# Two token tiles of the second batch turned on TensorE, and two GpSimd products moved ahead of five loads

## The chip, the cores and the metric

The kernel runs on one core of a Trainium2 chip. The metric is the device time of one execution in microseconds (us); lower is better. The core's engines are TensorE (PE in the profile; PEld is its weight loads), VectorE (DVE), ScalarE (ACT), GpSimd (POOL) and SyncE (SP, which only issues DMAs here). Each engine runs its own list of instructions in order and waits on semaphores for the others.

## The reference

Sliding-window attention with sink tokens, followed by a gated block over the whole sequence. There are 4 batches, 8 heads, 768 tokens, 64 values a head; each query sees the 127 keys before it, itself, and the first 4 keys.

```python
# attention, per batch and head
scores = (q @ k.T) / sqrt(64)
keep = (pos_k < 4) | ((pos_q - pos_k >= 0) & (pos_q - pos_k < 128))
a = softmax(where(keep, scores, -1e9))
x = a @ v                                  # heads side by side: (4, 768, 512)
# gated block
h = gelu_tanh(x @ w_in)                    # (4, 768, 1024)
u, v = h[..., :512], h[..., 512:]
v_n = (v - mean(v)) / sqrt(var(v) + 1e-6) * g_ln
v_s = einsum('ts,bsd->btd', w_sg, v_n) + b_sg[None, :, None]
out = x + (u * v_s) @ w_out
```

## The kernel before

All work is cut into small steps, each a Python function with a short name, and one string, `STEPS`, writes out by hand the order in which the steps are recorded. Each step puts its instructions at the end of its engine's list, so the string fixes the order on each engine and, between engines, what can overlap. A step reads `NAME.batch.index...`; a last letter A, D or P chooses ACT, DVE or POOL. The four batches are interleaved: while the gated block of one batch runs, the attention of the next runs beside it, and the loads of the one after that arrive.

A batch has 6 tiles of 128 tokens. The steps around the change are these (lines are those of the profile):

- `LQ`, `LK` (line 223) and `LVH` (line 272): loads of q, k and v, issued by GpSimd, converting to bf16. `LK.3.0` is the first token tile of k of batch 3; `LVH.2.0` is half of the heads of v of batch 2.
- `TK`, `EK` (lines 379, 197): k turned on TensorE, and copied from PSUM. `DQ`, `DK` (line 437): q and k turned by a transposing DMA that SP issues, two token tiles each.
- `QK.b.p.g` (line 480): scores of head pair p and token tiles 2g and 2g+1, into one of two score buffers (`sc`) in PSUM. `EX` (line 485): the exponential on ACT. `MK` (lines 492, 495, 498): the window mask, on DVE or, as two selects, on POOL.
- `AV.b.p.k` (lines 521, 525, 528): the value product of head pair p for half k of the tokens (three tiles), into one of four `mm` buffers in PSUM. `NR` (lines 537, 538): the division by the row sum, which writes `x_sb` in bf16.
- `XT`, `XE` (lines 547, 197): two token tiles of x turned on TensorE, eight 128x128 transposes into an `mm` buffer, then copied to `xT`. Batch 0 uses these throughout. `XD` (line 554): half of x, three token tiles, turned by a transposing DMA that SP issues. Batches 1 to 3 use it.
- `MV.b.g` (line 563): the product with the v half of `w_in` for token tiles 2g and 2g+1, into a score buffer; `GV` (line 567) its GELU. `MU`, `GU` (lines 607, 612): the same for the u half. `TL` (line 570): a tiny ACT instruction that has the GELU's table loaded.
- `BN`, `RS`, `NM`, `Z` (lines 579 to 583, 588, 591, 597, 600): mean and variance, the inverse root (on POOL), the offset, and the normalised tile.
- `SP.b.h.c` (line 627): the product over tokens with `w_sg`; `GT` (line 632) scale and bias on DVE; `GM` (line 637) the gate product u * v_s, on DVE or POOL.
- `OU` (line 644): the product with `w_out`; `RA` (line 648) the residual sum; `ST` (line 667) the store.

Buffers turn in rings: a step that takes a buffer waits until the last reader of its use before is done. Four `mm` buffers serve `AV`, `XT`, `TK`, `SP`, `SK` and `OU` in the order of recording; two `sc` buffers serve `QK`, `MV` and `MU`.

For batch 1, `XD.1.0` turns tiles 0 to 2 once `NR.1.0.0` to `NR.1.3.0` have written them, and `XD.1.1` turns tiles 3 to 5 once `NR.1.0.1` to `NR.1.3.1` have. `MV.1.0` and `MU.1.0` need tiles 0 and 1, `MV.1.1` tiles 2 and 3. In the order around the change, PE runs the value products `AV.1.0.1` to `AV.1.3.1`, the scores `QK.2.2.0` and `QK.2.3.0`, the output products `OU.0.1` and `OU.0.2`, then `MV.1.0`. SP issues `XD.1.0`, `XD.1.1`, then `DQ.2.1`, `DQ.2.2`, `DK.2.2`, `DK.3.0`, `DQ.3.0`.

Of the kernel before, what the change touches and what calls it, by code (L numbers as in the profile page):

```python
# [43 lines left out]
NM.1.1 Z.1.0.A LK.3.3 RS.1.2 OU.0.3 GU.1.2 NM.1.2 Z.1.1.D Z.1.2.D Z.1.4.D Z.1.3.A Z.1.5.D OU.0.4 QK.2.0.1 QK.2.1.1
RA.0.3 DK.3.0 SP.1.0.0 RA.0.4 EX.2.0.1 SP.1.0.1 SK.2.0 GT.1.0.0 DQ.3.0 EX.2.1.1 SX.2.0 GM.1.0.0.D SP.1.1.0 MK.2.0.1.P
GT.1.0.1 QK.2.2.1 ST.0.3 GT.1.1.0 QK.2.3.1 GM.1.0.1.P EX.2.2.1 AV.2.0.0 SP.1.1.1 MK.2.1.1.D EX.2.3.1 MK.2.2.1.P
NR.2.0.0 AV.2.1.0 QK.2.0.2 QK.2.1.2 EX.2.0.2 MK.2.3.1.P NR.2.1.0 SP.1.1.2 GT.1.1.1 EX.2.1.2 OU.0.5 MK.2.0.2.P GT.1.1.2
ST.0.0 ST.0.4 QK.2.2.2 RA.0.5 QK.2.3.2 MK.2.1.2.P EX.2.2.2 AV.2.2.0 AV.2.3.0 NR.2.2.0 SP.1.1.3 EX.2.3.2 NR.2.3.0
QK.3.0.0 MK.2.3.2.P QK.3.1.0 GT.1.1.3 XD.2.0 EX.3.0.0 AV.2.0.1 MK.2.2.2.D AV.2.1.1 EX.3.1.0 NR.2.0.1 AV.2.2.1
GM.1.1.3.P ST.0.1 NR.2.1.1 AV.2.3.1 ST.0.2 ST.0.5 GM.1.1.0.P NR.2.2.1 QK.3.2.0 QK.3.3.0 NR.2.3.1 EX.3.2.0 GM.1.1.2.P  # L50
SP.1.0.2 EX.3.3.0 XD.2.1 DQ.3.1 DK.3.1 SP.1.0.3 GT.1.0.2 MK.3.3.0.D MV.2.0 GM.1.0.2.P GM.1.1.1.D LK.3.4 LK.3.5 LQ.3.4
LQ.3.5 MK.3.0.0.D OU.1.3 LVH.3.0 GV.2.0 OU.1.4 RA.1.3 LVH.3.1 DK.3.2 DQ.3.2 OU.1.5 ST.1.3 RA.1.4 GT.1.0.3 MV.2.1 ST.1.4
MK.3.1.0.D KS.3 BN.2.0 GM.1.0.3.P MV.2.2 GV.2.1 BN.2.1 MU.2.1 GV.2.2 BN.2.2 RS.2.1 MU.2.0 GU.2.1 NM.2.1 RA.1.5 RS.2.2
MU.2.2 GU.2.0 NM.2.2 Z.2.4.D Z.2.5.D Z.2.0.A Z.2.1.D OU.1.0 GU.2.2 Z.2.2.D MK.3.2.0.D OU.1.1 RA.1.0 Z.2.3.D QK.3.0.1
QK.3.1.1 RA.1.1 SP.2.0.0 EX.3.0.1 EX.3.1.1 OU.1.2 MK.3.0.1.P GT.2.0.0 ST.1.5 VSM.3 ST.1.0 QK.3.2.1 ST.1.1 QK.3.3.1
EX.3.2.1 SP.2.1.0 GM.2.0.0.D MK.3.1.1.P RA.1.2 EX.3.3.1 SP.2.0.1 ST.1.2 MK.3.3.1.P QK.3.0.2 GT.2.0.1 QK.3.1.2 SK.3.0
EX.3.0.2 SX.3.0 SP.2.1.1 GT.2.1.0 MK.3.2.1.P EX.3.1.2 GM.2.1.0.D SP.2.1.2 GT.2.1.1 GM.2.0.1.D AV.3.0.0 MK.3.1.2.P
GT.2.1.2 AV.3.1.0 NR.3.0.0 AV.3.2.0 AV.3.3.0 MK.3.0.2.P NR.3.1.0 QK.3.2.2 QK.3.3.2 EX.3.2.2 SP.2.0.2 NR.3.2.0 NR.3.3.0
EX.3.3.2 SP.2.0.3 MK.3.2.2.P GT.2.0.2 XD.3.0 AV.3.0.1 GT.2.0.3 MK.3.3.2.P AV.3.1.1 NR.3.0.1 AV.3.2.1 GM.2.0.3.P
NR.3.1.1 AV.3.3.1 SP.2.1.3 GM.2.0.2.D GM.2.1.1.P NR.3.2.1 OU.2.0 NR.3.3.1 GT.2.1.3 XD.3.1 OU.2.1 RA.2.0 GM.2.1.3.P  # L60
OU.2.2 GM.2.1.2.D ST.2.0 RA.2.1 MV.3.0 RA.2.2 ST.2.1 OU.2.3 GV.3.0 OU.2.4 BN.3.0 MV.3.1 RA.2.3 RA.2.4 MV.3.2 ST.2.3
GV.3.1 ST.2.2 ST.2.4 BN.3.1 OU.2.5 GV.3.2 MU.3.2 BN.3.2 RS.3.1 MU.3.1 GU.3.2 NM.3.1 RS.3.2 NM.3.2 Z.3.0.D Z.3.1.A
MU.3.0 Z.3.2.D Z.3.3.A Z.3.4.A Z.3.5.D RA.2.5 ST.2.5 SP.3.1.0 GU.3.0 SP.3.1.1 GU.3.1 GT.3.1.0 SP.3.1.2 GM.3.1.0.D
# [11 lines left out]
def kernel(  # L75
# [474 lines left out]
        copy(e, xT.get(b)[:, 2 * g:2 * g + 2].rearrange("p t c i -> p (t c) i"), ps16(("x", b, g), 8))  # L550

    def XD(b, half):
        ts = slice(3 * half, 3 * half + 3)
        return nc.sync.dma_start_transpose(out=xT.get(b)[:, ts, :, :].rearrange("p t c i -> p (t c) i"),
                                           in_=x_sb[b][:, ts, :].rearrange("p t d -> p (t d)"))

# [159 lines left out]
```

## Time and profile before

| | |
|---|---|
| median of 3 runs | 156.38 us (155.83 to 157.84) |
| the profiled execution's own time | 156.0 us |
| its span in the profile | 154.3 us |
| TensorE clock granted | 1.00 |
| busy: PE, DVE, ACT, POOL | 93%, 79%, 64%, 64% |
| DMA traffic | 25.44 MB, mean 165 GB/s |

The span is what the profile covers, from the first to the last instruction; the execution's own time has a little more around it. Busy shares are means over the whole span. In a timeline row the first number is the start in us from the span's start, the second the length in us, then engine, line and operation, output and inputs; a bracket at the end tells how long the engine stood idle before it and who ended that. Matmul records overlap, since matmuls are pipelined. Rows of SPq and of GpSimd's DMA instructions show the issue of a DMA, not the moving of its data; "DMA to landing" is counted from the start of the issue.

### The profile page before, as it was taken

What the parts mean: (1) busy time and instruction counts of PE and PEld (TensorE: products, weight loads), DVE (VectorE), ACT (ScalarE), POOL (GpSimd) and SP (SyncE); (2) the same over time, 40 slices, a digit from 0 to 9 for tenths busy, and PEclk for the clock granted to TensorE, in tenths of its full rate; (3) what the DMA queues carried; (4) which work ended last, traced back from release to release, by engine and by line L of the source; (5) the groups of instructions that cost most, each with busy time, mean ns of one, the idle gap of its engine ahead of it and who ended that gap; (6) DMA issues with size and microseconds to landing.
All of it is one profiled execution on the core that took longest, in us unless ns stands there. A gap on an engine that the chain in (4) does not pass through costs nothing.

```text
span 154.3 us, 3696 instructions
## 1 busy us (share of the span) xinstructions
PE 143.3 (93%) x1460; PEld 92.1 (60%) x1471; DVE 122.2 (79%) x292; ACT 99.4 (64%) x111; POOL 98.7 (64%) x127
## 2 busy tenths in 40 slices
...
GB/s 162 280 357 150 150 193 207 170 189 213 142 139 141 191 157 130 208 154 145 127 155 219 181 283 174 157 156 157 307 168 19 87 238 0 207 66 7 0 224 184
DMA packets 89337, 25.44 MB, mean 165 GB/s; under 512 B 81828, under 2 KB 86184, under 8 KB 89320
## 3 DMA queue, kind: packets, MB, share of 16 engines
...
q8 instruction: 11, 0.18, 0.5%
q14 instruction: 6, 0.05, 0.1%
...
## 4 chain that ended last, share of the span: by engine, by line
PE 72%; DMA 16%; DVE 4%; SPq 3%; POOL 2%; issue 1%; DVEq 0%
PE mm L627 17%; PE sc L607 14%; PE sc L563 13%; PE mm L644 12%; DMA k<-in_k_dram 6%; DMA z<-in_q_dram 5%; PE sc L480 4%; DMA xT<-x_sb 4%; PE mm L521 3%; SPq L243 3%; PE mm L525 2%; PE mm L379 2%; PE mm L528 1%; PE mm L619 1%; DVE x_sb L538 1%
## 5 line engine op out<-in xcount | busy, mean ns | idle before, releaser
L485 ACT ACTIVATE P<-sc 128x1024 bf16<-128x1024 f32 (+1 forms) x48 | 43.6, 956 | 9.3 <-PE sc L480 9.1
L627 PE MATMUL mm<-wsgT,z 128*128 128x384 bf16 x192 | 34.3, 327 | 0.0
L627 PEld LDWEIGHTS <-z 128*128 128x128 bf16 x192 | 17.5, 98 | 12.0 <-issue 1.2
L563 PE MATMUL sc<-w_in_sb,xT 128*128 128x512 bf16 x93 | 21.9, 379 | 1.5 <-DMA xT<-x_sb 1.3
L632 DVE SCALAR_TENSOR_TENSOR gtmp<-mm,g_sb,b_bc 128x384 bf16<-128x384 f32 x32 | 19.2, 611 | 4.5 <-PE mm L627 4.2
L644 PE MATMUL mm<-w_out_sb,wsg_gated 128*128 128x512 bf16 x89 | 22.0, 379 | 0.4
L607 PE MATMUL sc<-xT,w_in_sb 128*128 128x256 bf16 x192 | 22.1, 273 | 0.0
L495 POOL TENSOR_SCALAR_AFFINE_SELECT P<-P 128x512 bf16<-128x512 bf16 x21 | 13.7, 651 | 13.0 <-ACT P L485 12.3
L637 POOL TENSOR_TENSOR wsg_gated<-gtmp,uT 128x384 bf16<-128x384 bf16 x15 | 14.5, 986 | 10.5 <-DVE gtmp L632 10.5
L579 DVE BATCH_NORM_STATS2 st<-vt 128x6 f32<-128x512 f32 x24 | 15.4, 682 | 7.2 <-ACT vt L567 7.1
L607 PEld LDWEIGHTS <-w_in_sb 128*128 128x128 bf16 x192 | 18.7, 98 | 3.0
L567 ACT ACTIVATE vt<-sc 128x1024 f32<-128x1024 f32 x12 | 12.3, 1024 | 11.3 <-PE sc L563 11.3
L538 DVE TENSOR_TENSOR x_sb<-mm,rcp 128x384 bf16<-128x384 f32 (+1 forms) x36 | 18.5, 513 | 1.2
L648 DVE TENSOR_TENSOR ot<-mm,x_sb 128x512 f32<-128x512 f32 x24 | 16.1, 683 | 2.4 <-PE mm L644 2.4
L223 POOL DMA_DIRECT2D k<-in_k_dram x18 | 16.4, 921 | 1.1 <-DMA v_sb<-in_v_dram 1.1
L588 POOL TENSOR_TENSOR rs<-rs,neg_half 128x4 f32<-128x4 f32 (+1 forms) x8 | 6.9, 867 | 15.3 <-DVE rs L583 14.1
L521 PE MATMUL mm<-v_sb,P 128*128 128x65 bf16 x192 | 16.2, 194 | 0.4 <-DVE x_sb L538 0.3
L223 POOL DMA_DIRECT2D q<-in_q_dram x18 | 16.4, 928 | 0.0
L563 PEld LDWEIGHTS <-xT 128*128 128x128 bf16 x96 | 9.2, 98 | 11.9 <-DMA xT<-x_sb 1.8
L521 PEld LDWEIGHTS <-P 128*128 128x128 bf16 x192 | 14.6, 97 | 2.4 <-DMA v_sb<-in_v_dram 0.5
L525 PE MATMUL mm<-v_sb,P 128*128 128x65 bf16 x160 | 15.5, 193 | 0.4 <-POOL P L498 0.4
L480 PE MATMUL sc<-qT,kT 64*128 64x128 bf16 (+1 forms) x256 | 14.6, 238 | 1.0 <-DVE qT L198 0.6
...
## 6 DMA issues: line engine op xcount, KB each, us to landing
...
```

The source lines that it names most:

```text
L223: return nc.gpsimd.dma_start(out=dst.rearrange("p (h d) -> p h d", h=H), in_=heads(src, b, i))
L480: nc.tensor.matmul(sc[:, hl, c:c + 128 * ni], at(kT, b)[rows, j, p, :], at(qT, b)[rows, i:i + ni, p, :], start=not biased, stop=(not biase ...
L485: nc.scalar.activation(out=P.new((b, p, g))[:, :, 0:w], in_=sc_ring[b, p, g][:, :, 0:w], func=AF.Exp, scale=scale)
L521: nc.tensor.matmul(av[:, il, hl, :], pt[:, hl, c:c + 128], vb[:, h, i, :], start=first, stop=False)
L525: nc.tensor.matmul(av[:, il, hl, :], pt[:, hl, c:c + 128], vb[:, h, i - 1, :], start=False, stop=(i < 2 and il == n - 1 and hl == 1))
L538: nc.vector.tensor_mul(x_sb.get(b)[:, i0:i0 + n, 128 * p:128 * (p + 1)].rearrange("p t (h d) -> p t h d", h=2), av[:, :, :, 0:Dh], rcp[:, ...
L563: nc.tensor.matmul(hp[:, jl, :], xT[b][:, 2 * g + jl, c, :], w_in_sb[:, c, d_half:2 * d_half], start=(c == 0), stop=(c == KD - 1))
L607: nc.tensor.matmul(hp[:, dc // 2, 256 * (dc % 2):256 * (dc % 2 + 1)], w_in_sb[:, c, 128 * dc:128 * (dc + 1)], xT[b][:, 2 * g:2 * g + 2, c, :],
L627: nc.tensor.matmul(ps[:, 0:NH], z[b][:, si, 128 * dc:128 * (dc + 1)], wsgT[:, si, NH * hf:NH * (hf + 1)], start=(si == 0), stop=(si == NT ...
L632: nc.vector.scalar_tensor_tensor(out=gtmp.new((b, hf, dc)), in0=mm_ring["g", b, hf, dc][:, 0:NH], scalar=g_sb[:, dc:dc + 1], in1=b_bc[:, N ...
L644: nc.tensor.matmul(ps, gated(b, hf)[:, dc, 128 * tl:128 * (tl + 1)], w_out_sb[:, dc, :], start=(dc == 0), stop=(dc == KU - 1))
L648: nc.vector.tensor_add(ot.new((b, t)), mm_ring["o", b, t], x_sb[b][:, t, :])
```

## The change

In batch 1, token tiles 0 and 1 of x are turned by `XT.1.0` on TensorE and copied by `XE.1.0` on ACT, and `XD.1.0` turns tile 2 alone. `XD.1.1` still turns tiles 3 to 5. `XT.1.0` stands behind `QK.2.3.0`. Both score steps `QK.2.2.0` and `QK.2.3.0`, which stood behind `AV.1.3.1`, now stand ahead of it, as does `XT.1.0`. On ACT, `XE.1.0` stands between `EX.2.2.0` and `EX.2.3.0`. On GpSimd, the gate products `GM.0.1.3` and `GM.0.1.1` stand directly behind `GM.0.1.2` and ahead of `LK.3.0`, `LK.3.1`, `LQ.3.0`, `LQ.3.1` and `LVH.2.0`; before, they stood behind those and `LVH.2.1`. The orders of DVE and of SP's issues stay as they were.

```diff
 ...
-RA.0.0 AV.1.0.1 XD.1.0 EK.2.1.A MK.1.3.2.P AV.1.1.1 NR.1.0.1 AV.1.2.1 EX.2.1.0 GM.0.1.2.P NR.1.1.1 AV.1.3.1 NR.1.2.1
-QK.2.2.0 LK.3.0 LK.3.1 LQ.3.0 LQ.3.1 LVH.2.0 QK.2.3.0 EX.2.2.0 OU.0.1 NR.1.3.1 EX.2.3.0 TL OU.0.2 XD.1.1 DQ.2.1 DQ.2.2
-DK.2.2 RA.0.1 MK.2.3.0.D MV.1.0 VSM.2 MU.1.0 GV.1.0 MK.2.1.0.D LVH.2.1 GM.0.1.3.P GM.0.1.1.P BN.1.0 MV.1.1 GU.1.0
+RA.0.0 AV.1.0.1 XD.1.0 EK.2.1.A MK.1.3.2.P AV.1.1.1 NR.1.0.1 AV.1.2.1 EX.2.1.0 QK.2.2.0 QK.2.3.0 XT.1.0 EX.2.2.0
+GM.0.1.2.P NR.1.1.1 AV.1.3.1 NR.1.2.1 GM.0.1.3.P GM.0.1.1.P LK.3.0 LK.3.1 LQ.3.0 LQ.3.1 LVH.2.0 OU.0.1 NR.1.3.1
+XE.1.0.A EX.2.3.0 TL OU.0.2 XD.1.1 DQ.2.1 DQ.2.2 DK.2.2 RA.0.1 MK.2.3.0.D MV.1.0 VSM.2 MU.1.0 GV.1.0 MK.2.1.0.D LVH.2.1
+BN.1.0 MV.1.1 GU.1.0
 ...
     def XD(b, half):
-        ts = slice(3 * half, 3 * half + 3)
+        ts = slice(2 if b == 1 and half == 0 else 3 * half, 3 * half + 3)
         return nc.sync.dma_start_transpose(out=xT.get(b)[:, ts, :, :].rearrange("p t c i -> p (t c) i"),
                                            in_=x_sb[b][:, ts, :].rearrange("p t d -> p (t d)"))
```

From `BN.1.0` on, the written order is the same in both.

More of the change, by code (lines that the diff above doesn't have):

```diff
@@ L39 @@
 NR.1.1.0 AV.1.2.0 AV.1.3.0 MK.1.0.2.P GT.0.1.3 QK.2.0.0 QK.2.1.0 NR.1.2.0 EX.2.0.0 OU.0.0 MK.1.2.2.P NR.1.3.0 TK.2.1
-RA.0.0 AV.1.0.1 XD.1.0 EK.2.1.A MK.1.3.2.P AV.1.1.1 NR.1.0.1 AV.1.2.1 EX.2.1.0 GM.0.1.2.P NR.1.1.1 AV.1.3.1 NR.1.2.1
-QK.2.2.0 LK.3.0 LK.3.1 LQ.3.0 LQ.3.1 LVH.2.0 QK.2.3.0 EX.2.2.0 OU.0.1 NR.1.3.1 EX.2.3.0 TL OU.0.2 XD.1.1 DQ.2.1 DQ.2.2
-DK.2.2 RA.0.1 MK.2.3.0.D MV.1.0 VSM.2 MU.1.0 GV.1.0 MK.2.1.0.D LVH.2.1 GM.0.1.3.P GM.0.1.1.P BN.1.0 MV.1.1 GU.1.0
-LQ.3.2 RA.0.2 LQ.3.3 MK.2.0.0.D MV.1.2 GV.1.1 MK.2.2.0.D KS.2 BN.1.1 MU.1.1 GV.1.2 BN.1.2 LK.3.2 RS.1.1 MU.1.2 GU.1.1
@@ L44 @@
[L44 to L63, printed above, removed]
@@ L64 @@
-GT.3.1.1 SP.3.1.3 GM.3.1.1.D GT.3.1.2 SP.3.0.0 GM.3.1.2.D SP.3.0.1 GT.3.0.0 GT.3.1.3 SP.3.0.2 GT.3.0.1 GM.3.1.3.P
-SP.3.0.3 GM.3.0.0.D GM.3.0.1.P GT.3.0.2 OU.3.3 GM.3.0.2.D GT.3.0.3 OU.3.4 GM.3.0.3.D RA.3.3 OU.3.0 RA.3.4 ST.3.3 OU.3.1
-RA.3.0 ST.3.4 OU.3.2 ST.3.0 RA.3.1 OU.3.5 ST.3.1 RA.3.2 ST.3.2 RA.3.5 ST.3.5
+RA.0.0 AV.1.0.1 XD.1.0 EK.2.1.A MK.1.3.2.P AV.1.1.1 NR.1.0.1 AV.1.2.1 EX.2.1.0 QK.2.2.0 QK.2.3.0 XT.1.0 EX.2.2.0
+GM.0.1.2.P NR.1.1.1 AV.1.3.1 NR.1.2.1 GM.0.1.3.P GM.0.1.1.P LK.3.0 LK.3.1 LQ.3.0 LQ.3.1 LVH.2.0 OU.0.1 NR.1.3.1
@@ new lines @@
+XE.1.0.A EX.2.3.0 TL OU.0.2 XD.1.1 DQ.2.1 DQ.2.2 DK.2.2 RA.0.1 MK.2.3.0.D MV.1.0 VSM.2 MU.1.0 GV.1.0 MK.2.1.0.D LVH.2.1
+BN.1.0 MV.1.1 GU.1.0 LQ.3.2 RA.0.2 LQ.3.3 MK.2.0.0.D MV.1.2 GV.1.1 MK.2.2.0.D KS.2 BN.1.1 MU.1.1 GV.1.2 BN.1.2 LK.3.2
+RS.1.1 MU.1.2 GU.1.1 NM.1.1 Z.1.0.A LK.3.3 RS.1.2 OU.0.3 GU.1.2 NM.1.2 Z.1.1.D Z.1.2.D Z.1.4.D Z.1.3.A Z.1.5.D OU.0.4
+QK.2.0.1 QK.2.1.1 RA.0.3 DK.3.0 SP.1.0.0 RA.0.4 EX.2.0.1 SP.1.0.1 SK.2.0 GT.1.0.0 DQ.3.0 EX.2.1.1 SX.2.0 GM.1.0.0.D
+SP.1.1.0 MK.2.0.1.P GT.1.0.1 QK.2.2.1 ST.0.3 GT.1.1.0 QK.2.3.1 GM.1.0.1.P EX.2.2.1 AV.2.0.0 SP.1.1.1 MK.2.1.1.D
@@ new lines @@
+EX.2.3.1 MK.2.2.1.P NR.2.0.0 AV.2.1.0 QK.2.0.2 QK.2.1.2 EX.2.0.2 MK.2.3.1.P NR.2.1.0 SP.1.1.2 GT.1.1.1 EX.2.1.2 OU.0.5
+MK.2.0.2.P GT.1.1.2 ST.0.0 ST.0.4 QK.2.2.2 RA.0.5 QK.2.3.2 MK.2.1.2.P EX.2.2.2 AV.2.2.0 AV.2.3.0 NR.2.2.0 SP.1.1.3
+EX.2.3.2 NR.2.3.0 QK.3.0.0 MK.2.3.2.P QK.3.1.0 GT.1.1.3 XD.2.0 EX.3.0.0 AV.2.0.1 MK.2.2.2.D AV.2.1.1 EX.3.1.0 NR.2.0.1
+AV.2.2.1 GM.1.1.3.P ST.0.1 NR.2.1.1 AV.2.3.1 ST.0.2 ST.0.5 GM.1.1.0.P NR.2.2.1 QK.3.2.0 QK.3.3.0 NR.2.3.1 EX.3.2.0
+GM.1.1.2.P SP.1.0.2 EX.3.3.0 XD.2.1 DQ.3.1 DK.3.1 SP.1.0.3 GT.1.0.2 MK.3.3.0.D MV.2.0 GM.1.0.2.P GM.1.1.1.D LK.3.4
@@ new lines @@
+LK.3.5 LQ.3.4 LQ.3.5 MK.3.0.0.D OU.1.3 LVH.3.0 GV.2.0 OU.1.4 RA.1.3 LVH.3.1 DK.3.2 DQ.3.2 OU.1.5 ST.1.3 RA.1.4 GT.1.0.3
+MV.2.1 ST.1.4 MK.3.1.0.D KS.3 BN.2.0 GM.1.0.3.P MV.2.2 GV.2.1 BN.2.1 MU.2.1 GV.2.2 BN.2.2 RS.2.1 MU.2.0 GU.2.1 NM.2.1
+RA.1.5 RS.2.2 MU.2.2 GU.2.0 NM.2.2 Z.2.4.D Z.2.5.D Z.2.0.A Z.2.1.D OU.1.0 GU.2.2 Z.2.2.D MK.3.2.0.D OU.1.1 RA.1.0
+Z.2.3.D QK.3.0.1 QK.3.1.1 RA.1.1 SP.2.0.0 EX.3.0.1 EX.3.1.1 OU.1.2 MK.3.0.1.P GT.2.0.0 ST.1.5 VSM.3 ST.1.0 QK.3.2.1
+ST.1.1 QK.3.3.1 EX.3.2.1 SP.2.1.0 GM.2.0.0.D MK.3.1.1.P RA.1.2 EX.3.3.1 SP.2.0.1 ST.1.2 MK.3.3.1.P QK.3.0.2 GT.2.0.1
@@ new lines @@
+QK.3.1.2 SK.3.0 EX.3.0.2 SX.3.0 SP.2.1.1 GT.2.1.0 MK.3.2.1.P EX.3.1.2 GM.2.1.0.D SP.2.1.2 GT.2.1.1 GM.2.0.1.D AV.3.0.0
+MK.3.1.2.P GT.2.1.2 AV.3.1.0 NR.3.0.0 AV.3.2.0 AV.3.3.0 MK.3.0.2.P NR.3.1.0 QK.3.2.2 QK.3.3.2 EX.3.2.2 SP.2.0.2
+NR.3.2.0 NR.3.3.0 EX.3.3.2 SP.2.0.3 MK.3.2.2.P GT.2.0.2 XD.3.0 AV.3.0.1 GT.2.0.3 MK.3.3.2.P AV.3.1.1 NR.3.0.1 AV.3.2.1
+GM.2.0.3.P NR.3.1.1 AV.3.3.1 SP.2.1.3 GM.2.0.2.D GM.2.1.1.P NR.3.2.1 OU.2.0 NR.3.3.1 GT.2.1.3 XD.3.1 OU.2.1 RA.2.0
+GM.2.1.3.P OU.2.2 GM.2.1.2.D ST.2.0 RA.2.1 MV.3.0 RA.2.2 ST.2.1 OU.2.3 GV.3.0 OU.2.4 BN.3.0 MV.3.1 RA.2.3 RA.2.4 MV.3.2
```

5 lines of the change are left out of this document (added).

## Prediction

> **What bounds the kernel now.** I read the page's busy shares first, then TensorE's busy time by stretch, then the waits, then the order of time around the edited steps. The page:
>
> ```profile
> span 154.3 us, 3696 instructions
> PE 143.3 (93%) x1460; PEld 92.1 (60%) x1471; DVE 122.2 (79%) x292; ACT 99.4 (64%) x111; POOL 98.7 (64%) x127
> ```
>
> TensorE (PE) is the bound on average. An average hides stages, so here is PE alone in stretches cut at 62.88 us, where the first matmul of MV.1.0 starts, and at 75.68, where the gate product of batch 1 starts. Columns: busy us, instructions, granted clock, DMA share, GB/s.
>
> ```profile
> 50.00:62.88 12.88, 10.88 (x165) 1.00 1.95 162
> 62.88:75.68 12.80, 12.75 (x92) 1.00 1.97 156
> 75.68:90.00 14.32, 14.21 (x205) 1.00 1.54 187
> 90.00:110.00 20.00, 19.89 (x139) 1.00 1.67 185
> ```
>
> From 62.88 on PE has 0.05 to 0.11 us of idle time in a stretch; the 2.00 us it lacks lie ahead of 62.88. Nothing later waits for anything but PE, so work that brings MV.1.0 forward brings the end forward, and no more can be had than the idle time ahead of it. Which waits these are, by the waits view and the chain that ended last:
>
> ```profile
> PE sc L563 <- DMA xT<-x_sb: 1.3, 1, 1.3
> PE mm L525 <- POOL P L498: 0.4, 1, 0.4
> ...
> 56.02 6.81 DMA xT<-x_sb
> ```
>
> MV.1.0 (line 563) waits for xT, which the transposing DMA XD.1.0 fills: issued at 56.02, in at 62.83. The value product AV.1.3.1 (line 525) waits for a mask that GpSimd applies. The order of time on the engines, before:
>
> ```profile
> 57.37 0.82 ACT L485 ACTIVATE P<-sc 128x768 bf16<-128x768 f32 x1
> 58.12 0.63 POOL L498 TENSOR_SCALAR_AFFINE_SELECT P<-P 128x512 bf16<-128x512 bf16 x1
> 58.22 0.20 PE L521 MATMUL mm<-v_sb,P 128*128 128x65 bf16 x1
> 58.81 0.20 PE L525 MATMUL mm<-v_sb,P 128*128 128x65 bf16 x1 [0.39 <-POOL P L498]
> 59.24 0.50 PE L480 MATMUL sc<-qT,kT 64*128 64x256 bf16 x8
> 59.62 1.51 ACT L485 ACTIVATE P<-sc 128x768 bf16<-128x768 f32 x2 [1.43 <-PE sc L480]
> 60.77 0.81 PE L644 MATMUL mm<-w_out_sb,wsg_gated 128*128 128x512 bf16 x3
> 61.15 1.28 ACT L570 ACT_TABLE_LOAD   x1
> 62.88 1.90 PE L563 MATMUL sc<-w_in_sb,xT 128*128 128x512 bf16 x8 [1.30 <-DMA xT<-x_sb]
> 66.36 3.62 PE L563 MATMUL sc<-w_in_sb,xT 128*128 128x512 bf16 x16
> ```
>
> The reader is to see two holes in PE (58.22 to 58.81, and the end of OU.0.2 to 62.88) and, in the same stretch, ScalarE (ACT) idle for 1.43 us ahead of 59.62.
>
> **The change, part by part.** *MV.1.0's wait goes.* Its two token tiles now come from XT.1.0 and XE.1.0, not from XD.1.0. The idle record says 1.30 us. Counted from start to start it is more: three of OU.0.2's matmuls span 0.81 and one lasts 0.38, so each takes 0.215; the last begins at 61.20, the next could begin at 61.41, and 62.88 is 1.47 later. Gain 1.30 to 1.47.
>
> *AV.1.3.1's wait goes.* The score steps QK.2.2.0 and QK.2.3.0 and the new XT.1.0 stand ahead of it, so PE works while GpSimd finishes the mask at 58.75. Start to start 58.22 to 58.81 less one 0.03 step is 0.56, by the idle record 0.39. The score steps must not wait instead: QK.2.3.0 needs the PSUM buffer that the exponential at 57.37 frees at 58.19, and PE reaches it after 58.4.
>
> *XT.1.0 is added*: eight 128x128 transposes on PE. Batch 0 has the same step; in the chain, and in the list of that line's matmuls:
>
> ```profile
> 28.30 0.45 PE mm L547 x8
> ...
> L547 PE MATMUL mm<-iden,x_sb x24: 218/219/219, 22.4 to 28.5; 128*128 128x128 bf16 x24
> ```
>
> In a row of eight they cost 0.45, though each is recorded at 219 ns: they overlap. Cost 0.45; if they did not overlap, 8 x 0.219 = 1.75. Its data (the first half of x) was complete when XD.1.0 issued at 56.02, so it waits for nothing.
>
> The Trainium skill (TensorE: Matmul & The Clock Gate, Part 4: PE-mode transpose) speaks against the change: it puts a transpose at about 275 ns in a kernel's context. Eight of them would be an estimated 2.2 us by that figure, and would eat the whole gain; the 0.45 of the chain's row disagrees, and I go by the row.
>
> *XE.1.0 is added on ACT*, the copy of PSUM to xT:
>
> ```profile
> L197 ACT COPY xT<-mm x2: 1007/1010/1012, 24.2 to 29.3; 128x1024 bf16<-128x1024 bf16 x2
> ```
>
> One us. ACT's 1.43 us hole covers it: QK.2.2.0 now runs about 1 us earlier, its exponential starts near 58.6 instead of 59.62 and ends near 59.4, XE.1.0 runs 59.4 to 60.4, EX.2.3.0 to 61.15, and the table load begins where it did, at 61.15. MV.1.0 will ask for xT near 61.4: 1.0 us to spare. Cost nothing. Without that cover it would be 1.0.
>
> *The lead at MV.1.0.* By idle records 1.30 + 0.39 - 0.45 = 1.24; start to start 1.47 + 0.56 - 0.45 = 1.58. I take the middle, 1.4: MV.1.0 starts at 61.5.
>
> *What is late next: XD.1.1.* The second transposing DMA (three tiles, as before) can only follow AV.1.3.1, which now has 0.50 + 0.45 of other work ahead and 0.56 less wait: 0.4 later. SP's issues, and time to landing, first of all six then of XD.1.1 alone:
>
> ```profile
> 56.02 1.50 SPq L554 DMA_TRANSPOSE xT<-x_sb  x1
> 60.23 2.59 SPq L554 DMA_TRANSPOSE xT<-x_sb  x1
> ...
> DMA to landing us min/median/max: 3.7/3.9/6.2
> ...
> DMA to landing us min/median/max: 6.2/6.2/6.2
> ```
>
> XD.1.1 issues at 60.6. Its first reader is the second half of MV.1.1: 66.36 + 4 x 0.215 - 1.4 = 65.8. So 5.2 us are there. At 3.7 it costs nothing, at 6.2 it lands at 66.8 and costs 1.0. I take nothing: the 6.2 was met behind a full-sized XD.1.0 (in until 62.83; XD.1.1's own issue dragged to 62.82), and XD.1.0 now moves a third of the bytes. XD.1.0's single tile is needed only by MV.1.1's first half at 65.0, 9 us after its issue, against 6.81 now. DQ.2.1, DQ.2.2 and DK.2.2 stand behind XD.1.1 on SP and move with it, 0.4 later at most.
>
> *GpSimd's gate products ahead of loads.* GpSimd's (POOL's) order before:
>
> ```profile
> 59.58 1.81 POOL L223 DMA_DIRECT2D k<-in_k_dram  x2
> 61.38 1.77 POOL L223 DMA_DIRECT2D q<-in_q_dram  x2
> 63.11 2.86 POOL L272 DMA_DIRECT2D v_sb<-in_v_dram  x2
> 65.94 1.84 POOL L637 TENSOR_TENSOR wsg_gated<-gtmp,uT 128x384 bf16<-128x384 bf16 x2
> 67.67 1.83 POOL L223 DMA_DIRECT2D q<-in_q_dram  x2
> 69.46 0.90 POOL L223 DMA_DIRECT2D k<-in_k_dram  x1
> 71.20 1.03 POOL L588 TENSOR_TENSOR rs<-rs,neg_half 128x4 f32<-128x4 f32 x1 [0.83 <-DVE rs L583]
> 73.20 0.71 POOL L588 TENSOR_TENSOR rs<-rs,neg_half 128x2 f32<-128x2 f32 x1
> ```
>
> The two products (1.84) move from 65.94 to 59.6; the five loads, and LVH.2.1 behind them, issue 1.84 later, and from 67.7 on the order is as before. The products' reader OU.0.3 comes behind MU.1.2 and gains nothing. Of the loads the tightest I can see is LVH.2.1, read by AV.2.2.0; the two v loads from issue to landing, and that product's first matmuls:
>
> ```profile
> DMA to landing us min/median/max: 10.9/13.5/16.2
> ...
> 84.54 0.27 PE L521 MATMUL mm<-v_sb,P 128*128 128x65 bf16 x3
> ```
>
> Issued at 64.5, in at 80.7 at the slowest; 1.84 later is 82.5, wanted at 84.54 - 1.4 = 83.1. Covered by 0.6; cost nothing, at the far end 0.6 if its queue adds over 1.2.
>
> *RS.1.1, RS.1.2 and the normalised tiles.* POOL's loads end at 70.36 as before, so RS.1.1, which had 0.83 us of idle time ahead of it, can come forward by 0.8 and not by 1.4; RS.1.2 follows it, and so do the Z steps on VectorE (DVE):
>
> ```profile
> 74.02 1.91 DVE L600 TENSOR_SCALAR z<-vt,rs,nmr 128x512 bf16<-128x512 f32 x4
> 75.68 2.12 PE L627 MATMUL mm<-wsgT,z 128*128 128x384 bf16 x12
> ```
>
> Z's last tile was ready at 75.93 and becomes ready at 75.1. The sixth matmul of SP.1.0.0 wants it at 75.68 + 5 x 0.18 - 1.4 = 75.2 (2.12 over 12). Just in time: cost 0 to 0.2, I take 0.1.
>
> **The sum.** 1.47 + 0.56 - 0.45, set at 1.4, less 0.1: the span goes from 154.3 to 153.0. The profiled execution took 156.0 in all, 1.7 around the span, so 154.7 by its own scale. The runs shown have a median of 156.38, 0.38 above that execution; I put 0.3 of it back: 155.0.
>
> **The rivals.** *The lead is partly given back.* XD.1.1 lands between 65.8 and 67.2, or LVH.2.1 late, or the Z steps at 0.2: 0.5 to 1.2 of 1.4 goes, 155.5 to 156.2. For it: XD.1.1's own 6.2. Against: its handicaps shrink. This also holds the case in which transposes on PE don't overlap, the skill's rule at the row's price: 1.75 - 0.45 = 1.3 goes and 156.3 results; the row makes it 2 in 100.
>
> *Slower: XD.1.1 runs into the k loads.* LK.3.0 and LK.3.1 now issue at 61.4 and 62.3 and move their data just when XD.1.1 does.
>
> ```profile
> DMA to landing us min/median/max: 4.3/4.8/5.2
> ```
>
> That is these two loads before, issued to landed; LK.3.1 would be in at 62.3 + 5.2 = 67.5. If XD.1.1 lands behind it, at 68.0, MV.1.1 stalls 2.2 us, the lead is overdrawn by 0.8, and the time is 157.2. It decides from 6.6 us of XD.1.1's issue to landing. For it: DMA share is high in this stretch (1.95 above). Against: no xT row is over 6.2, and the loads come late enough for XD.1.1 to start alone.
>
> The Trainium skill (DMA: Bandwidth & Descriptors, Queues, rings and completion order) says that each DMA engine takes turns between its queues packet by packet. By that rule the loads would slow XD.1.1 rather than hold it back whole, which favours the middle case over this one; whether it does is not shown by a row here.
>
> *More than forecast.* With 2.03 of start-to-start waits gone, 0.45 paid and the queues lighter, 154.2 to 153.9. PE's fullness after 62.88 allows no more.
>
> *The change doesn't do what it says*: MV.1.0 would still wait for XD.1.0. The changed build's order lists only ACT as what MV.1.0's first weight load waits for; under 1 in 100.
>
> **How the numbers follow.** Forecast 0.62, partly given back 0.21, slower 0.12, more than forecast 0.05. The likeliest case gives 155.0. The range is 153.9 (more than forecast) to 157.0 (most of the slower case). 2%, about what a measurement of this kernel can tell from no change, is 3.1 us: below 153.25 lies more than PE's holes allow (0.02); over 159.5 takes two late transfers one behind the other (0.04).
>
> **What would show it.** Right: MV.1.0's first matmul near 61.5 with no wait on xT's DMA; eight L547 transposes near 58.7 in 0.45; XE.1.0 ended by 60.5; the table load at 61.15; no PE idle time over 0.2 at MV.1.1; every later PE row 1.2 to 1.4 earlier. Wrong: a PE wait on xT's DMA inside MV.1.1, on v_sb, on qT ahead of batch 3's first scores, or L627 waiting for z.

## The result and the profile after

| | before | changed |
|---|---|---|
| median | 156.27 us (155.83 to 157.84, 4 runs) | 160.12 us (159.03 to 160.87, 4 runs) |
| profiled execution, span | 156.0, 154.3 us | 160.87, 159.1 us |
| TensorE clock granted | 1.00 | 0.984 |

The ratio is 1.028, with a 95% interval of 1.022 to 1.034: the changed kernel is slower by 2.8%. (A ratio leaves disturbed executions out and so can differ a little from the quotient of two medians.)

The page of the changed kernel, as far as it answers to that of before:

```profile
span 159.1 us, 3713 instructions
PE 144.6 (91%) x1468; PEld 93.1 (58%) x1479; DVE 122.4 (77%) x292; ACT 100.0 (63%) x112; POOL 98.7 (62%) x127
PEclk9999999999999999999999789999999999999998
```

The eight new matmuls last 0.45 us together, yet PE is busy 1.3 us longer: the 7 and the 8 in the row of the clock, some 87 to 95 us in, say where. To see where the span grew, both traces are cut at the same four events: the start of ACT's copy of `kT` (`EK.2.1.A`, the last large event before the edited steps), the first matmul of `MV.1.0`, the first of `SP.1.0.0`, and the first of `MV.2.0`. PE by stretch: from and to, length, busy us and matmuls, granted clock, DMA share, GB/s. First the changed kernel:

```profile
57.66:62.56 4.90, 4.85 (x82) 1.00 1.16 77
62.56:75.35 12.79, 12.74 (x92) 1.00 1.62 135
75.35:96.50 21.15, 17.53 (x215) 0.92 1.45 181
96.50:159.10 62.60, 58.48 (x466) 0.99 0.75 133
```

The same stretches before, with the second of them already among the prediction's rows:

```profile
56.46:62.88 6.42, 4.68 (x75) 1.00 1.91 149
75.68:91.65 15.97, 15.87 (x215) 1.00 1.48 208
91.65:154.30 62.65, 58.47 (x466) 1.00 0.77 135
```

The sum closes. This execution reaches the first event 1.20 us later, though nothing ahead of it was changed (over all profiles of this study it lies between 55.5 and 57.7 us, so no single span is better than a microsecond). The first stretch is 1.52 shorter: that is the lead. The second is as long as before, the fourth too. The third is 5.18 longer, and its two parts can be read in the row: 215 matmuls in both, but 17.53 us busy against 15.87, so 1.66 more at a granted clock of 0.92, and 3.62 idle against 0.10, so 3.52 more. 1.20 - 1.52 - 0.01 + 5.18 - 0.05 = 4.80, which is 159.1 - 154.3. From the first event to the end it is 101.5 us against 97.8, 3.7 more; the medians lie 3.85 apart.

The waits view and the chain that ended last of the changed kernel name what the idle time waits for; in the second line the load's issue begins at 67.58 and it is in 20.46 us later. The third is the time to landing of both halves of batch 2's v:

```profile
PE mm L521 <- DMA v_sb<-in_v_dram: 3.5, 2, 2.8
...
67.58 20.46 DMA v_sb<-in_v_dram
...
DMA to landing us min/median/max: 14.2/17.3/20.5
```

The long wait is that of `AV.2.2.0` for `LVH.2.1`, the second half of v; the short one, 0.71, is that of `AV.2.0.0` for `LVH.2.0`, the first. Before, the two loads landed 16.2 and 10.9 us after their issue and nothing waited. The timelines of the changed kernel, PE and ACT, then POOL, then PE again, where the prediction's steps can be looked up:

```profile
59.84 0.62 PE L547 MATMUL mm<-iden,x_sb 128*128 128x128 bf16 x8
60.30 0.19 PE L521 MATMUL mm<-v_sb,P 128*128 128x65 bf16 x1
60.50 1.01 ACT L197 COPY xT<-mm 128x1024 bf16<-128x1024 bf16 x1
62.24 1.28 ACT L570 ACT_TABLE_LOAD   x1
62.56 1.89 PE L563 MATMUL sc<-w_in_sb,xT 128*128 128x512 bf16 x8
...
60.06 2.65 POOL L637 TENSOR_TENSOR wsg_gated<-gtmp,uT 128x384 bf16<-128x384 bf16 x3
62.66 1.83 POOL L223 DMA_DIRECT2D k<-in_k_dram  x2
...
80.41 0.27 PE L521 MATMUL mm<-v_sb,P 128*128 128x65 bf16 x3 [0.71 <-DMA v_sb<-in_v_dram]
88.09 0.27 PE L521 MATMUL mm<-v_sb,P 128*128 128x65 bf16 x3 [2.77 <-DMA v_sb<-in_v_dram]
```

`MV.1.0` at 62.56 has no wait left. GpSimd's three products come first and its k loads start at 62.66, where it was 59.58: 1.84 by the order and 1.2 by the later start. PE stands for 0.71 us ahead of `AV.2.0.0` and for 2.77 ahead of `AV.2.2.0`. PE by stretch of 2 us around the long stand, same columns as above:

```profile
86.00:88.00 2.00, 0.00 (x0) 1.00 2.39 155
88.00:90.00 2.00, 1.91 (x28) 0.82 1.63 104
90.00:92.00 2.00, 2.00 (x24) 0.50 0.40 70
```

The stand costs twice. From 89.3 to 92.7 the granted clock is 0.50, and there, with no wait at all, PE makes 24 matmuls in 2 us.

### The profile page after: what moved, and what is told of

It is laid out like the page before. It is cut to its first block, busy times and chain, and to the rows that moved or that the text cites. A ratio compares the mean times of both kernels' runs of the same rounds, so it can differ in the third digit from the quotient of the medians.

```text
span 159.1 us, 3713 instructions
## 1 busy us (share of the span) xinstructions
PE 144.6 (91%) x1468; PEld 93.1 (58%) x1479; DVE 122.4 (77%) x292; ACT 100.0 (63%) x112; POOL 98.7 (62%) x127
## 4 chain that ended last, share of the span: by engine, by line
PE 52%; DMA 24%; POOL 13%; DVE 5%; issue 2%; ACT 2%; SPq 1%; DVEq 0%; POOLq 0%
DMA v_sb<-in_v_dram 19%; PE mm L627 12%; PE mm L644 10%; PE sc L563 9%; PE sc L607 8%; DMA uT<-in_q_dram 4%; PE sc L480 4%; POOL q L223 3%; PE mm L521 3%; POOL k L223 3%; PE mm L525 2%; DVE q L198 2%; PE mm L528 2%; POOL v_sb L272 2%; POOL wsg_gated L637 2%
## 5 line engine op out<-in xcount | busy, mean ns | idle before, releaser
L627 PE MATMUL mm<-wsgT,z 128*128 128x384 bf16 x192 | 35.0, 330 | 0.1
L521 PE MATMUL mm<-v_sb,P 128*128 128x65 bf16 x192 | 16.8, 197 | 3.5 <-DMA v_sb<-in_v_dram 3.5
L525 PE MATMUL mm<-v_sb,P 128*128 128x65 bf16 x160 | 16.1, 197 | 0.0
L644 PEld LDWEIGHTS <-wsg_gated 128*128 128x128 bf16 x96 | 9.3, 98 | 10.9 <-DMA w_out_sb<-in_moe_w_out_dram 0.9
```

Of the source, the lines that this page charges most:

```text
L521: nc.tensor.matmul(av[:, il, hl, :], pt[:, hl, c:c + 128], vb[:, h, i, :], start=first, stop=False)
L525: nc.tensor.matmul(av[:, il, hl, :], pt[:, hl, c:c + 128], vb[:, h, i - 1, :], start=False, stop=(i < 2 and il == n - 1 and hl == 1))
L627: nc.tensor.matmul(ps[:, 0:NH], z[b][:, si, 128 * dc:128 * (dc + 1)], wsgT[:, si, NH * hf:NH * (hf + 1)], start=(si == 0), stop=(si == NT ...
L644: nc.tensor.matmul(ps, gated(b, hf)[:, dc, 128 * tl:128 * (tl + 1)], w_out_sb[:, dc, :], start=(dc == 0), stop=(dc == KU - 1))
```

## The experiments

All but the second start from the changed kernel. Each ratio is against executions of the kernel before that were taken beside that experiment's own (their medians are 155.36 to 155.78 us), so ratios can be compared between experiments, medians only roughly. For all but the sixth, the same four stretches, in us, and the time from the `kT` copy to the landing of `LVH.2.1`, which takes the start-up of an execution out of the comparison (before 24.3, changed 30.4); of TensorE's part alone it is the second profile:

| kernel | to MV.1.0 | to SP.1.0.0 | to MV.2.0 | to the end | LVH.2.1 |
|---|---|---|---|---|---|
| before | 6.42 | 12.80 | 15.97 | 62.6 | 24.3 |
| changed | 4.90 | 12.79 | 21.15 | 62.6 | 30.4 |
| changed, again | 4.77 | 12.79 | 20.85 | 62.6 | 30.0 |
| TensorE's part alone | 4.87 | 13.74 | 15.97 | 62.6 | 25.6 |
| GpSimd's part alone | 5.48 | 12.80 | 16.53 | 62.6 | 27.9 |
| one gate product moved | 4.77 | 13.67 | 16.09 | 62.6 | 27.6 |
| hole filled | 4.77 | 12.79 | 20.03 | 62.7 | 29.9 |
| stores behind XD.2.0 | 4.77 | 12.79 | 17.15 | 65.1 | 26.9 |
| v first | 4.77 | 14.95 | 23.34 | 62.6 | 20.7 |
| four tiles on TensorE | 5.22 | 13.46 | 15.97 | 63.1 | 26.4 |
| four tiles, one product | 5.22 | 12.79 | 16.15 | 63.2 | 26.8 |

**1. TensorE's part alone.** The two gate products go back behind the loads.

```diff
-... NR.1.2.1 GM.0.1.3.P GM.0.1.1.P LK.3.0 ...  MK.2.1.0.D LVH.2.1 BN.1.0 ...
+... NR.1.2.1 LK.3.0 ...  MK.2.1.0.D LVH.2.1 GM.0.1.3.P GM.0.1.1.P BN.1.0 ...
```

> The change with the two GpSimd products put back behind LVH.2.1; XT.1.0, XE.1.0, the one-tile XD.1.0 and the two early score steps stay. Theory A (the products ahead of the loads make the v loads late): LVH.2.1 lands by 82 us of the span, no wait of TensorE on v_sb over 0.3 us, granted clock 1.00, and the lead of 1.2 to 1.4 us at MV.1.0 reaches the end: 154.6 to 155.4 us. Theory B (with XD.1.0 cut to one tile the transposing DMAs of q and k run ahead of the loads, and that makes the v loads late): still slower than before, 158 to 160 us, v_sb waited for by over 2 us.

Median 156.6 us (155.17 to 160.37, ten executions), ratio 1.006 (1.001 to 1.011). Nearly the whole loss is gone with the gate products put back, so it hangs on GpSimd's order. But the lead did not reach the end either. The execution profiled here took 160.37 us, 3.8 more than the median; in it `MV.1.1` waits 3.25 us for `XD.1.1`, which lands 8.4 us after its issue. Nothing more is rested on it, and the kernel was profiled once more:

> The kernel of pe_only again, one look: its first profile had TensorE waiting 3.25 us inside MV.1.1 for XD.1.1 (8.4 us from issue to landing, beside the k and q loads). Theory H (whether XD.1.1 is held back is drawn anew in each execution, by which of the two queues' data comes first, and most executions are spared): XD.1.1 lands within 6.5 us of its issue, no wait over 0.5 us in MV.1.1, span 153 to 155 us. If it is held back each time: again 3 us of wait there, and span over 157 us.

155.33 us, one execution. PE by stretch from the `kT` copy to `SP.1.0.0`, the wait, and the chain's row of the same execution:

```profile
56.38:61.25 4.87, 4.87 (x83) 1.00 1.25 88
61.25:74.99 13.74, 12.97 (x94) 1.00 2.03 146
...
PE sc L563 <- DMA xT<-x_sb: 0.8, 1, 0.8
...
60.54 5.94 DMA xT<-x_sb
```

The lead is there, 1.5 us. Then `MV.1.1` waits 0.8 for `XD.1.1`, which lands 5.94 us after its issue (within the 6.5 expected, but the wait is over the 0.5), and the second stretch is 0.95 longer. Of v nothing waits. So in this execution most of the lead is paid out to the transposing DMA that comes next.

**2. GpSimd's part alone.** The kernel before, with only the two products ahead of the loads.

```diff
-... QK.2.2.0 LK.3.0 ...  LVH.2.1 GM.0.1.3.P GM.0.1.1.P BN.1.0 ...
+... QK.2.2.0 GM.0.1.3.P GM.0.1.1.P LK.3.0 ...  LVH.2.1 BN.1.0 ...
```

> The kernel before with only the two GpSimd products moved ahead of LK.3.0; MV.1.0 still waits for the three-tile XD.1.0. Theory A: the v loads land as late as in the changed kernel (LVH.2.1 at 85 to 88 us); TensorE reaches AV.2.2.0 1.2 to 1.4 us later than there, so it waits 1.5 to 2.5 us for v_sb and loses some clock behind it: 158.0 to 160.0 us. Theory B: the loads move by the 1.84 us of the two products alone, LVH.2.1 lands at 82 to 83 us, ahead of AV.2.2.0 at 84.5: 156.0 to 156.8 us.

Median 156.24 us (154.66 to 157.77), ratio 1.006 (1.002 to 1.011). Neither expectation was met. The waits, and the chain's row of the load:

```profile
PE mm L521 <- DMA v_sb<-in_v_dram: 2.2, 3, 1.1
PE sc L563 <- DMA xT<-x_sb: 0.4, 1, 0.4
...
66.46 18.14 DMA v_sb<-in_v_dram
```

v is late with this part alone, 3.6 us later from the `kT` copy than before, for an issue 1.84 later; but only one of the three waits of the first line lies there, 0.72 at `AV.2.2.0`, and the third stretch grows by 0.56 only. And `MV.1.0`'s wait on the whole `XD.1.0` fell from 1.30 to 0.41, presumably since the k loads that it shared the DMA engines with now come later: 0.94 gained in the first stretch. The two parts do not add up in time, 0.6% each and 2.8% together, because v has some slack (before, it was in at 80.7 and read at 84.54) and the lead uses it up: together v comes 6.1 later while PE asks for it 1.5 sooner. In landing time, 1.3 and 3.6 make 4.9 of the 6.1.

**3. Is it the clock?** Thirteen idle matmuls of 512 columns stand ahead of `AV.2.2.0`, in the buffer that it takes.

```diff
-... EX.2.2.2 AV.2.2.0 ...
+... EX.2.2.2 HM.13 AV.2.2.0 ...
```

> The changed kernel with 13 idle matmuls of 512 columns on zeros (2.8 us) written ahead of AV.2.2.0 into its own PSUM buffer, so that TensorE is not idle while it waits for the v load; nothing of the result changes. Theory C (of the 4.5 us lost some 1.5 us is the lower clock after the idle time: granted 0.82, 0.50 and 0.83 in three stretches of 2 us behind it): granted clock 1.00 from 88 us on, 158.2 to 159.0 us. Theory D (the clock record behind the wait costs nothing, all of the loss is the wait itself and its followers): 160.0 us or more, as the changed kernel.

Median 158.63 us (158.04 to 159.26), ratio 1.021 (1.013 to 1.029). PE by stretch of 2 us behind the filled hole, to be held against the rows of the changed kernel above:

```profile
88.00:90.00 2.00, 2.00 (x34) 1.00 0.74 47
90.00:92.00 2.00, 2.00 (x58) 1.00 0.77 113
```

v comes as late as in the changed kernel (29.9 us from the `kT` copy), and the clock stays at 1.00: 58 matmuls in the stretch where there were 24. The third stretch is 0.8 to 1.1 shorter than in the two profiles of the changed kernel. The ratio is 0.7% lower than the changed kernel's 1.028, but the two intervals overlap, so the gain rests on the stretches. That much of the half clock's cost comes back; it is a part of the loss, not its cause.

**4. v ahead of all other loads.** 

```diff
-... GM.0.1.1.P LK.3.0 LK.3.1 LQ.3.0 LQ.3.1 LVH.2.0 OU.0.1 ...  MK.2.1.0.D LVH.2.1 BN.1.0 ...
+... GM.0.1.1.P LVH.2.0 LVH.2.1 LK.3.0 LK.3.1 LQ.3.0 LQ.3.1 OU.0.1 ...  MK.2.1.0.D BN.1.0 ...
```

> The changed kernel with LVH.2.0 and LVH.2.1 issued ahead of LK.3.0, LK.3.1, LQ.3.0 and LQ.3.1, the two products still ahead of all. If the wait on v_sb is all that the change costs (theory A or B alike): LVH.2.1 lands by 78 us, no wait on v_sb, and 154.6 to 155.6 us unless the k and q tiles of batch 3, now 2.9 us later, become the next thing late. If the whole queue of loads is behind (theory E: too many bytes between 66 and 88 us beside the transposing DMAs, whichever load comes last is late): DK.3.0 or DQ.3.0 lands after 86 us, QK.3.0.0 waits for it, 157 to 160 us.

Median 163.46 us (162.02 to 163.94), ratio 1.051 (1.041 to 1.061): slower than either expectation (at worst 160 us, by late tiles of k and q), and by another way. The waits:

```profile
DVE nmr L591 <- POOL rs L588: 9.8, 4, 5.2
...
POOL k L223 <- DMA v_sb<-in_v_dram: 6.9, 3, 3.6
...
PE mm L627 <- DVE z L600: 4.3, 1, 4.3
```

v lands at 76.3 and no PE wait on it is long. But POOL's own later load issues `LK.3.2` and `LK.3.3` stand until the two halves of v have landed (2.40 and 3.64 of the 6.9 us; the third stand is of an earlier batch), behind them on POOL stand the inverse roots of `RS.1.1` and `RS.1.2`, behind those the offsets and the Z tiles on DVE, and behind those `SP.1.0.0` (4.3 us). The granted clock is then 0.50 for 10.2 us. So a later load's issue can stand on GpSimd until an earlier load has landed, and the arithmetic behind it stands too.

**5. The stores out of v's way.** SP's three stores of batch 0's results go behind `XD.2.0`.

```diff
-... QK.2.2.1 ST.0.3 GT.1.1.0 ...  GT.1.1.2 ST.0.0 ST.0.4 QK.2.2.2 ...  XD.2.0 EX.3.0.0 ...
+... QK.2.2.1 GT.1.1.0 ...  GT.1.1.2 QK.2.2.2 ...  XD.2.0 ST.0.3 ST.0.0 ST.0.4 EX.3.0.0 ...
```

> The changed kernel with the three stores ST.0.3, ST.0.0 and ST.0.4 issued behind XD.2.0 and not ahead of it. Theory F (engines of the DMA take one packet of each queue in turn; beside the 2 KB packets of these stores the loads fall from 410 packets a us beside the transposing DMAs, and 1200 alone, to 165, and that is the last of what makes LVH.2.1 late): from the last transposing DMA on, near 82 us, the loads run at 1200 packets a us, LVH.2.1 lands 1.5 to 2.5 us earlier than in the changed kernel, at 85 to 86.5 us, and 1 to 2.5 us of the loss come back: 1.0 to 2.0% slower than before instead of 2.8%. Rival G (the stores do not matter, the queue of loads is late as a whole): LVH.2.1 lands where it did, 87 us or later, and 2.5 to 3% slower than before.

Median 159.45 us (158.7 to 161.46), ratio 1.025 (1.020 to 1.030). First what the DMA queues of the changed kernel move in single microseconds: packets, MB, share of 16 engines. q0 carries GpSimd's loads, q1 SP's DMAs. From 76 to 77, where SP's transposing `DQ.3.0` runs:

```profile
q0 software_dynamic: 426, 0.05, 82.6%
q1 hardware_dynamic: 425, 0.10, 80.5%
```

From 84 to 85, where the stores run:

```profile
q1 hardware_dynamic: 164, 0.30, 91.0%
q0 software_dynamic: 164, 0.02, 31.8%
```

And from 87 to 88, where the loads are alone:

```profile
q0 software_dynamic: 1224, 0.15, 242.6%
```

In the first two stretches the two queues take turns one packet for one, whatever the packets' size. The loads move 1224 packets in a microsecond alone, a third of it beside transposes, and a seventh beside the stores, whose packets are 1.8 KB on average and take the longer. This is the rule of the Trainium skill (DMA: Bandwidth & Descriptors, Queues, rings and completion order) that each DMA engine takes turns between its queues packet by packet; these rows agree with it. Before, the stores' packets moved at the same place of the order, from 84 to 85, when `LVH.2.1` had been in since 80.7:

```profile
q1 hardware_dynamic: 162, 0.30, 89.5%
q0 software_dynamic: 164, 0.02, 31.2%
```

Now the kernel with the stores moved, from 83 to 84, and its two v loads from issue to landing:

```profile
q0 software_dynamic: 1225, 0.15, 242.9%
...
DMA to landing us min/median/max: 14.4/15.8/17.2
```

This execution began at the same 57.7 us as the changed kernel's, and `LVH.2.1` lands at 84.58 and not at 88.04. So 3.5 of the 6.1 us by which v was late hang on the stores. The third stretch falls from 21.15 to 17.15. Two things show in the traces beside this. `LVH.2.0` gains nothing: it takes 14.4 us to land, 14.2 in the changed kernel and 10.9 before, and is in at 80.4, ahead of the stores' packets. So the lateness begins ahead of the stores, and they keep a part of it from being made up. And a load's landing is counted in sixteen parts: in the changed kernel fifteen of `LVH.2.1`'s are in at 86.60 and the last at 88.04 (85.85 and 86.92 in its second profile); with the stores moved the last two come at 84.56 and 84.58. In experiments 3, 7 and 8 one part lags by 0.9 to 1.1 us too; why it does is not shown.

The landing is earlier than expected, but the time is above the 1.0 to 2.0% expected. The stores now stand between `XD.2.0` and what follows on SP:

```profile
PE sc L563 <- DMA xT<-x_sb: 1.6, 1, 1.6
```

`MV.2.1` waits 1.6 for `XD.2.1`, and the last stretch is 2.5 longer.

**6. v between k and q.**

```diff
-... LK.3.1 LQ.3.0 LQ.3.1 LVH.2.0 OU.0.1 ...  MK.2.1.0.D LVH.2.1 BN.1.0 ...
+... LK.3.1 LVH.2.0 LVH.2.1 LQ.3.0 LQ.3.1 OU.0.1 ...  MK.2.1.0.D BN.1.0 ...
```

> The changed kernel with LVH.2.0 and LVH.2.1 ahead of LQ.3.0 and LQ.3.1, behind LK.3.0 and LK.3.1; the loads start as late as in the changed kernel, only their order differs. If the order in the queue decides (LVH.2.1 has 2,048 packets fewer ahead of it, at 410 packets a us 5 us): LVH.2.1 lands by 82 us, TensorE waits for v_sb under 0.3 us, the clock stays at 1.00 and the lead at MV.1.0 reaches the end: 0.3 to 1.0% faster than before. If something else of batch 3 takes the place of v (DQ.3.0 waits for LQ.3.0 and LQ.3.1, and QK.3.0.0 for it; or POOL's load issue waits for an earlier load to land, and RS.1.2 behind it): 1 to 5% slower than before, with a wait on qT ahead of 86 us or of L627 on z.

Four executions: 156.03, 156.46, 159.70 and 160.02 us; ratio 1.006 (1.000 to 1.011). It is not faster than before as expected, and its profile, of the execution of 160.02 us, settles nothing: there PE waits 2.6 us for `DQ.3.0`, the q that went behind v. Whether a wait for q takes the place of the one for v is left open.

**7. One gate product moved, not two.**

```diff
-... GM.0.1.3.P GM.0.1.1.P LK.3.0 ...  LVH.2.1 BN.1.0 ...
+... GM.0.1.3.P LK.3.0 ...  LVH.2.1 GM.0.1.1.P BN.1.0 ...
```

> The changed kernel with one product ahead of the loads (GM.0.1.3) and GM.0.1.1 back behind LVH.2.1: the loads issue 0.9 us later than before instead of 1.8. If the loss grows out of the delay of the loads (theory A, in proportion or steeper): LVH.2.1 lands between 82 and 86 us, v_sb waited for by 0 to 1.2 us: 0 to 1.2% slower than before. If the two edits hurt each other in some way that does not go by the delay: 2.5% or more slower, as the changed kernel.

Median 155.58 us (154.40 to 156.53), ratio 1.001 (0.995 to 1.007): no difference from before. The waits view:

```profile
PE mm L521 <- DMA v_sb<-in_v_dram: 0.3, 1, 0.3
```

Half the delay on GpSimd costs 0.3 at `AV.2.2.0` and 0.1 in the third stretch; the whole costs 5.2 there. From the `kT` copy `LVH.2.1` lands after 25.6, 27.6 and 30.0 to 30.4 us with none, one and two of the products ahead of the loads, 2.0 and 2.4 to 2.8 for 0.92 of issue each. The cost is no straight line in the issue time: it sets in when v's slack is gone, is steeper than one for one, in part because the loads then meet the stores, and takes the clock with it when the stand is long.

**8 and 9. The transposing DMA made lighter.** Tiles 0 to 3 are turned on TensorE, `XD.1.0` goes, `XD.1.1` turns tiles 4 and 5; the gate products stand behind the loads, or (ninth) one of them ahead.

```diff
-        ts = slice(2 if b == 1 and half == 0 else 3 * half, 3 * half + 3)
+        ts = slice(4 if b == 1 else 3 * half, 3 * half + 3)
-... AV.1.0.1 XD.1.0 EK.2.1.A ...  OU.0.2 XD.1.1 ...  MK.2.3.0.D MV.1.0 ...
+... AV.1.0.1 EK.2.1.A ...  OU.0.2 XT.1.1 XD.1.1 ...  MK.2.3.0.D XE.1.1.D MV.1.0 ...
```

> Four token tiles of x on TensorE: the two products behind LVH.2.1 as before, XT.1.0 and XE.1.0 as in the changed kernel, XT.1.1 and XE.1.1 (on VectorE) added behind OU.0.2, XD.1.0 gone, XD.1.1 turning tiles 4 and 5 alone, first read by MV.1.2 near 67 us. If the wait in MV.1.1 for XD.1.1 (0.8 us in the better look at pe_only) is what keeps the lead of 1.5 us from the end: no wait of line 563 on xT's DMA, MV.1.0 0.45 us later than in pe_only, LVH.2.1 in by 82 us, and 0.5 to 1.0% faster than before. If the lead is lost further on as well (Z behind POOL's loads, v_sb): same as before within 0.3%.

> The same with GM.0.1.3 ahead of LK.3.0, so the loads issue 0.9 us later. By the reading that delayed loads lose what TensorE gains: LVH.2.1 at 83 to 84.5 us, 0 to 1 us of wait on v_sb, 0.2 to 0.8% slower than four_pe. If the delay of 0.9 us is free: as four_pe.

156.54 us (155.38 to 160.63), ratio 1.006 (1.002 to 1.009), and 156.09 (154.62 to 159.30), ratio 1.003 (1.000 to 1.007), in twelve executions each. Neither beats the kernel before, and the ninth is not the slower of the two as expected. The eighth's wait and its chain's row:

```profile
PE sc L563 <- DMA xT<-x_sb: 0.5, 1, 0.5
...
60.35 6.96 DMA xT<-x_sb
```

Two tiles need 6.96 us from issue to landing where three needed 5.94 in the first experiment and 4.4 in the changed kernel. By the other profiles the order of issue fits better than the size: three tiles took 3.7 to 4.4 us where GpSimd issued the first of the five loads 0.7 to 1.1 us behind `XD.1.1` (changed kernel twice, experiments 2 to 5), and 5.9 to 8.4 where it did so 0.2 to 1.0 us ahead (before, experiment 1 twice, experiment 7), as with these two tiles. The sixth experiment's 5.8, with the loads 0.8 behind, does not fit, and no run changed the company alone; so this is a reading and not shown.

**10. The changed kernel once more.**

> The changed kernel once more, one look. If the late v load is a property of the order and not of the one execution that was profiled: LVH.2.1 lands after 86 us, TensorE idle for 2 to 3.5 us at AV.2.2.0, granted clock 0.5 for some 3.4 us about 4 us after that idle time begins, 158.5 to 161 us.

159.73 us, one execution. The third stretch by its PE row, the wait, and the load:

```profile
74.51:95.36 20.85, 17.55 (x216) 0.92 1.46 183
...
PE mm L521 <- DMA v_sb<-in_v_dram: 4.5, 3, 2.5
...
66.65 20.26 DMA v_sb<-in_v_dram
```

The late load, the stand of 2.5 and the clock of 0.92 repeat, in an execution that began 0.7 sooner. It is not a chance of one trace.

## Why the prediction was wrong, step by step

- **The lead: right.** Forecast 1.4, measured 1.52 in the profile and 1.55 to 1.65 in the others with the same edit. `XT.1.0` was put at 0.45: from 59.84 to the next matmul at 60.30 it is 0.46, so eight transposes overlap, against the Trainium skill's 275 ns each (TensorE: Matmul & The Clock Gate, Part 4: PE-mode transpose), as the prediction had it. `XE.1.0` ended at 61.51 and the table load began at 62.24, which are 60.31 and 61.04 when the 1.20 later start is taken off; forecast were 60.4 and 61.15.
- **"What is late next: XD.1.1": right for this kernel, by the reason that stood under a rival.** Taken was no cost, because `XD.1.0` had become small; under "Slower" it said that the loads come late enough for `XD.1.1` to start alone. From issue to landing of `XD.1.1` in the changed kernel:

```profile
DMA to landing us min/median/max: 4.4/4.4/4.4
```

Nothing waited. The rival "XD.1.1 runs into the k loads" did not come true: the first k load was issued 0.8 us behind `XD.1.1`. In the first experiment, where it was issued 0.9 ahead, the wait was 0.8, though `XD.1.0` was as small. So the move of the products hid the cost that the prediction weighed most.
- **The normalised tiles: right but for a tenth.** Forecast 0 to 0.2. From `MV.1.0` to the first matmul of `SP.1.0.0` it is 12.79 us against 12.80; but the tile that comes last is wanted inside `SP.1.0.0`, which spans 2.38 us against 2.12 (2.28 in the second profile): 0.16 to 0.26.
- **"Issued at 64.5, in at 80.7; 1.84 later is 82.5 ... covered by 0.6; cost nothing, at the far end 0.6 if its queue adds over 1.2": the step that failed.** It carried a shift of the issue one for one to the landing. But the 16.2 us from issue to landing hold turns taken with SP's queue, as experiment 5 shows, and such a time changes when the load meets other neighbours. It was 20.46. The load landed 6.1 later from the same event, not 1.84. `LVH.2.0`, which had more cover and was not looked at, landed 5.2 later and was waited for too. Together they cost 3.5 us of idle time and 1.7 of half clock, where 0.6 was the far end. PE's rows by stretch of 2 us carry the DMA share and GB/s in their last two columns, and show where the shift may have grown. Changed kernel:

```profile
60.00:62.00 2.00, 1.95 (x28) 1.00 0.23 18
62.00:64.00 2.00, 2.00 (x11) 1.00 0.51 99
```

and before:

```profile
60.00:62.00 2.00, 1.52 (x7) 1.00 0.82 139
62.00:64.00 2.00, 1.12 (x6) 1.00 1.76 214
```

In these 4 us the DMA engines moved 234 KB (18 and 99 GB/s, 2 us each), before 706 KB. The 1.2 us later start of this execution is a part of the difference: counted from the `kT` copy, from 2 to 6 us behind it, it is 188 KB against 568 (47 and 142 GB/s). The reading is that both edits, the smaller `XD.1.0` and the later loads, emptied the same stretch, and that what was not moved there was still to come when the stores did. That the stores matter is shown by experiment 5; the part of the empty stretch is argued, not shown by a run of its own.
- **The rule that was at hand.** The prediction named the packet-by-packet rule for `XD.1.1` only, and said that no row showed it. The queues' packets of the kernel before, from 78 to 79 us, show it, in the view of DMA queues that was not cut so finely:

```profile
q1 hardware_dynamic: 413, 0.11, 79.8%
q0 software_dynamic: 413, 0.05, 79.6%
```

One for one again, while v was on its way; the rule spoke on v, where the cover was thinnest.
- **The price of a stand.** PE idle time was counted one for one. The stand of 2.77 brought 3.4 us at half clock behind it, 1.7 us; stands of 0.7 us, there and in the second experiment, and of 1.6 in the fifth brought none.
- **The list of signs** named "a PE wait ... on v_sb" and that is what the trace shows; the chance put on slower than 159.5, "two late transfers one behind the other", was 0.04. It was two late transfers, but both halves of v, which stood behind one and the same delay.

What stays open: GpSimd's part alone issues `LK.3.0` at 61.53 and the changed kernel's second profile at 61.73, nearly the same, and yet v lands 2.3 us later in the latter. The stores' place and the full `XD.1.0` differ between them; no run told these apart. Nor did a run show by itself what makes `LVH.2.0` late. And the runs with v on time have profiles 0.1 to 0.7 us shorter from the `kT` copy to the end than before, but ratios up to 1.006; why the lead does not show in the medians beyond `XD.1.1`'s wait was not settled.
